# Attention halves that cross a token block are multiplied with v in two pieces

## The chip, the cores and the metric

The kernel runs on one core of one Trainium2 chip. The metric is the device time of one execution in microseconds (us). It was 1517.95 us in the middle of three runs (1516.6 to 1519.84). A core has five engines with instruction queues of their own: TensorE (PE; its weight loads stand apart as PEld), VectorE (DVE), ScalarE (ACT), GpSimd (POOL) and SyncE (SP). They wait for one another by semaphores.

## The reference

```python
# q, k, v: (8 batches, 8 heads, 576 tokens, 64), k and v averaged over groups of 8 tokens: 72 keys
k_p = k.reshape(B, H, Sp, pool, D).mean(axis=3)
v_p = v.reshape(B, H, Sp, pool, D).mean(axis=3)
attn = softmax(scale * q @ k_p.T)            # per head, 576 x 72
x = (attn @ v_p)                             # to (4608 tokens, 512)
h = ((x @ w1) * (x @ w2)) @ w3               # 512 -> 1024 -> 1024
x2 = h @ w_out                               # 1024 -> 512
out = relu(x2 @ w_in) ** 2 @ w_out2          # 512 -> 2048 -> 512
```

## The kernel before

The tokens of all eight batches stand behind one another, 4608 in all. The dense layers take them in nine blocks of `TB = 512` (the loop over `i` near L1383). For each block `stage_ab(i, u)` makes eight times 24 products of 512 columns (tile `ps_w`: x with w1 and with w2), and `stage_w(i, u)` eight times 12 more (tile `acc`). Every operand is a pair of rounded halves, high and low, so that a product takes three matmuls (`mm3`). When all blocks are through, from some 810 us on, the second network follows (tiles `ps_a` to `ps_d`, `ps_h`, `o`).

Attention makes the x of these blocks while they are worked on. A batch has 576 tokens, so its borders fall elsewhere than those of the blocks. It is cut into five tiles of 128, 128, 128, 96 and 96 tokens (`QT`), and these into two halves of 256 and 320 tokens (`HALF`). `pe_s` makes the scores of a tile, `pe_t` turns the softmax, and `pe_av(b, hf, hp)` multiplies a half of a batch with v for one of four pairs of heads: four matmuls as wide as the half (three at L194, one at L533) into one buffer of the tile `ps_av`. ACT copies the result out as the high part of x (L546), and DVE takes the difference as the low part (L549), each once for every block that the half touches. `ps_av`, `ps_s`, `ps_t` and `ps_kt` share a pool of two PSUM buffers (`ps_at`), so that a product has to wait until the one two places ahead in that pool is read out.

`build_tasks` writes the order of these tasks as a list. `attend` is called at every tick of the dense work, about once in six matmuls, and takes tasks from the head of the list against a credit. A task has conditions: `("v", b)` says that v of the batch is split, and `("ab", last - 2)` that the block two before the last one that this half reaches is through `stage_ab`, since x has buffers for two blocks. While the head of the list has to wait, nothing behind it runs, and the credit stops at 3. Where a block is to begin and its x isn't there, `until(lambda: tokens_ready(...))` ticks until the tasks have been issued. A scheduler then moves instructions within a queue, but the order of a list's tasks stays.

v is summed over groups of eight tokens on DVE (L329, and L325 for the rows left over) into `vp` and `v5`, and then split by `cut` and `cut_odd` (L362, L363, L375) into `vl` and `vr`, which `pe_av` loads as weights. Each batch's steps for k and v wait in the list `back["kv"]`, of which `load_back` takes one at a tick. `load_v(b + 1)` is called behind the last product of batch b, and both the sums and the split follow from there.

Of the kernel before, what the change touches and what calls it, by code (L numbers as in the profile page):

```python
# [35 lines left out]
def attn_moe_moe2_kernel(  # L36
# [320 lines left out]
    def load_v(b):  # L357


        def parted(hi, lo, src, row):  # L360

            nc.scalar.activation(hi, src, ACTF.Copy, scale=row)  # L362
            nc.vector.scalar_tensor_tensor(  # L363
                lo, src, row, f32(hi), op0=ALU.mult, op1=ALU.subtract)

        def cut():
            for x in range(2):
                parted(vl[:, 0, :, x, :], vl[:, 1, :, x, :], vp, rows[:, x:x + 1])

        def cut_odd():  # L370
            vo = vr.rearrange("p (a b) t d -> p b a t d", a=2)[:, :, :, 1]
            for x in range(2):
                row = rows[:RB, 2 + x:3 + x]
                parted(vo[:RB, x], vo[2 * RB:, x], v5, row)
                nc.scalar.activation(vo[RB:2 * RB, x], v5, ACTF.Copy, scale=row)  # L375
            done.add(("v", b))

        return kv_parts(v, b, lambda j: vp[:, j, :], [cut, cut_odd])

    def pe_kt(b, part):  # L380

# [140 lines left out]
        dl = rem[RB:2 * RB, :, c0:c0 + n]  # L522
        nc.vector.tensor_sub(dl, ps[RB:2 * RB, :2, :n], f32(dl))

    def pe_av(b, hf, hp):
        hi, lo, rem = atts[b, hf]
        s0 = QT[HALF[hf][0]][0]
        w = sum(QT[i][1] for i in HALF[hf])
        ps = ps_at.tile([P, TB], F32, tag="at", name="ps_av")
        st = [vl[:, i, hp].rearrange("p a d -> p (a d)") for i in range(2)]  # L530
        for m in mm3(ps[:, :w], [(st, [t[:, hp, :w] for t in (hi, lo)])], last=False):
            m()
        nc.tensor.matmul(  # L533
            ps[:, :w], vr[:, hp].rearrange("p a d -> p (a d)"), rem[:, hp // 2, :w],
            start=False, stop=True)
        t0 = b * S + s0
        pieces = []
        o = 0
        while o < w:
            blk, c = divmod(t0 + o, TB)  # L540
            n = min(w - o, TB - c)
            pieces.append((blk, c, o, n))
            o += n

        for blk, c, o, n in pieces:
            nc.scalar.copy(xt_tile(blk, hp)[:, 0, c:c + n], ps[:, o:o + n])  # L546
        for blk, c, o, n in pieces:
            t = xt_tile(blk, hp)
            nc.vector.tensor_sub(t[:, 1, c:c + n], ps[:, o:o + n], f32(t[:, 0, c:c + n]))  # L549
        done.add(("av", b, hf, hp))  # L550

    NG = B * len(QT)

    def s_end(hf):
        return QT[HALF[hf][-1]][0] + QT[HALF[hf][-1]][1]

    def build_tasks(first_k, first_v):
# [4 lines left out]
        pend = []  # L562
        ride = []

        def put(fn, need=()):
            with_it = ride[:]
            del ride[:]
            order.append((need, [*with_it, fn]))

        def close():  # L570
            ends.add(len(order))
# [13 lines left out]
            close()  # L585

        def sc(g):
            alone = not pend
            for half in range(2):
                put(lambda half=half: pe_s(g, half))  # L590
                put_pend()
                if not alone:
                    close()
            close()
# [31 lines left out]
        for g in range(NG):  # L626
            b, i = divmod(g, len(QT))
            hf = 0 if i in HALF[0] else 1

            if g + 1 != len(QT):  # L630
                ahead_of(g)
            if i == HALF[hf][0]:
                put_all()
            for part in range(2):
                put(lambda g=g, part=part: pe_t(g, part))
            close()
            if g == 0:
                for fn in first_v:
                    put(fn)
                    close()  # L640
            if i == HALF[hf][-1]:
                need = [("v", b)]

                last = (b * S + s_end(hf) - 1) // TB
                if last >= 2:
                    need.append(("ab", last - 2))
                for hp in range(NP):
                    def av(b=b, hf=hf, hp=hp):
                        pe_av(b, hf, hp)
                        if hf == 1 and hp == NP - 1 and b + 1 < B:  # L650
                            load_v(b + 1)
                    pend.append((av, need))
                if b < EARLY:
                    put_all()
            if g + 1 == len(QT):
                ahead_of(g)
        put_all()
        return [(need, fns, n + 1 in ends) for n, (need, fns) in enumerate(order)]

    credit = [0.0]  # L660
    rate = [0.0]
# [2 lines left out]
    def attend():  # L664
# [2 lines left out]
        if credit[0] < visit[0]:  # L667
            return
        while credit[0] >= 1.0 and tasks:
            need, fns, ends = tasks[0]  # L670
            if not all(x in done for x in need):
                credit[0] = min(credit[0], 3.0)
                return
            tasks.pop(0)
            for fn in fns:
                fn()
            credit[0] -= 1.0
            if ends and visit[0] > 1:
                return

# [1 line left out]

    def tokens_ready(n):

        b, s = divmod(n, S)
        halves = [(bb, h) for bb in range(b) for h in range(2)]
        if s:
            halves.append((b, 0))
            if s > QT[HALF[1][0]][0]:
                halves.append((b, 1))  # L690
        return all(("av", bb, h, hp) in done for bb, h in halves for hp in range(NP))


    wt = {}
# [822 lines left out]
```

## Time and profile before

| | |
|---|---|
| median of three runs | 1517.95 us |
| the profiled execution: its own time | 1518.94 us |
| its span, from the first to the last instruction | 1517.2 us |
| PE busy | 1478.1 us (97%), 6752 matmuls |
| DVE, ACT, POOL busy | 997.3, 796.5, 81.8 us |
| mean granted TensorE clock | 0.996 of 2.4 GHz |

The profile is of one execution. A matmul's record holds the time that its columns take and the time until its last result is written, so that records of consecutive matmuls overlap; how fast PE goes is read from their starts. Times in the rows below are us from the span's start, if nothing else is said.

### The profile page before, as it was taken

What the parts mean: (1) busy time and instruction counts of PE and PEld (TensorE: products, weight loads), DVE (VectorE), ACT (ScalarE), POOL (GpSimd) and SP (SyncE); (2) the same over time, 40 slices, a digit from 0 to 9 for tenths busy, and PEclk for the clock granted to TensorE, in tenths of its full rate; (3) what the DMA queues carried; (4) which work ended last, traced back from release to release, by engine and by line L of the source; (5) the groups of instructions that cost most, each with busy time, mean ns of one, the idle gap of its engine ahead of it and who ended that gap; (6) DMA issues with size and microseconds to landing.
All of it is one profiled execution on the core that took longest, in us unless ns stands there. A gap on an engine that the chain in (4) does not pass through costs nothing.

```text
span 1517.2 us, 21303 instructions
## 1 busy us (share of the span) xinstructions
PE 1478.1 (97%) x6752; PEld 1199.4 (79%) x6752; DVE 997.3 (66%) x1798; ACT 796.5 (53%) x1953; POOL 81.8 (5%) x145
## 2 busy tenths in 40 slices
PE   5899999999999999999999999999999999999998
PEld 3457788888888887878888888888888888888887
DVE  7988766867666467484256487659675967576542
ACT  6876555546445436463146674456445644554431
POOL 1011111111110011100000000000000000000000
PEclk9999999999999999999999999999999999999999
DMA  9544766758577557475349877778777877798752
GB/s 288 200 140 116 198 184 158 217 141 236 144 202 205 167 138 213 128 243 171 97 146 324 284 201 240 207 208 233 232 208 209 230 207 208 208 271 283 210 161 88
DMA packets 292783, 301.34 MB, mean 199 GB/s; under 512 B 119360, under 2 KB 184896, under 8 KB 292672
## 3 DMA queue, kind: packets, MB, share of 16 engines
q1 hardware_dynamic: 287488, 290.54, 65.8%
q10 hardware_dynamic: 5184, 9.44, 1.7%
q8 instruction: 55, 0.90, 0.3%
q14 instruction: 56, 0.46, 0.1%
HBM read 243.27 MB, written 56.62 MB: 198 GB/s over the span
## 4 chain that ended last, share of the span: by engine, by line
PE 64%; DVE 3%; ACT 3%; issue 1%; DMA 1%; SPq 0%; DVEq 0%; ACTq 0%
PE o L1228 18%; PE ps_w L194 13%; PE acc L194 7%; PE ps_c L1126 5%; PE ps_a L1126 5%; PE ps_d L1126 5%; PE ps_h L194 3%; PE o L194 3%; PE ps_b L1126 3%; PE ps_av L194 1%; PE ps_s L468 1%; DVE gt L122 1%; ACT x2o L121 0%; ACT gs L1134 0%; ACT gt L121 0%
## 5 line engine op out<-in xcount | busy, mean ns | idle before, releaser
L1228 PE MATMUL o<-gt,un 128*128 128x512 f32 x1344 | 329.2, 390 | 0.4
L1228 PEld LDWEIGHTS o<-gt,un 128*128 128x128 f32 x1344 | 251.9, 188 | 54.5 <-DVE gt L122 2.1
L122 DVE TENSOR_TENSOR gt<-gs,gt 128x512 fp32r<-128x512 f32 x240 | 164.5, 688 | 178.9 <-ACT gt L121 177.5
L194 PE MATMUL ps_w<-x,wt 128*128 128x512 f32 x960 | 236.5, 396 | 1.6 <-ACT asb L849 0.7
L121 ACT CAST gt<-gs 128x512 fp32r<-128x512 f32 x240 | 148.5, 620 | 155.0 <-PE o L1228 88.2
L194 PE MATMUL acc<-gt,Wt 128*128 128x512 f32 x864 | 217.8, 396 | 0.0
L194 PEld LDWEIGHTS ps_w<-x,wt 128*128 128x128 f32 x960 | 177.5, 189 | 38.5 <-DVE wt L1319 1.5
L194 PEld LDWEIGHTS acc<-gt,Wt 128*128 128x128 f32 x864 | 160.3, 189 | 31.2
L194 PE MATMUL ps_w<-x,un 128*128 128x512 f32 x768 | 184.7, 393 | 0.0
L194 PEld LDWEIGHTS ps_w<-x,un 128*128 128x128 f32 x768 | 142.6, 188 | 29.0
L485 ACT ACTIVATE att<-ps_s,mx 128x72 f32<-128x72 f32 (+1 forms) x320 | 97.6, 324 | 50.6 <-DVE mx L483 49.7
L1133 ACT ACTIVATE r<-r 128x512 f32<-128x512 f32 x96 | 60.7, 632 | 117.5 <-DVE r L1163 117.0
L853 DVE TENSOR_TENSOR gf<-asb,ps_w 128x512 f32<-128x512 f32 x72 | 49.3, 684 | 84.7 <-PE ps_w L194 84.0
L1126 PE MATMUL ps_d<-x2o,un 128*128 128x512 f32 x384 | 97.4, 389 | 0.0
L1126 PE MATMUL ps_a<-x2o,un 128*128 128x512 f32 x384 | 97.4, 389 | 0.0
L1126 PE MATMUL ps_c<-x2o,un 128*128 128x512 f32 x384 | 97.4, 389 | 0.0
L1134 ACT ACTIVATE gs<-r 128x512 f32<-128x512 f32 x144 | 89.9, 629 | 1.9 <-ACT r L1133 0.2
L121 ACT CAST gt<-gf 128x512 fp32r<-128x512 f32 x72 | 44.9, 624 | 85.6 <-DVE gf L853 85.6
L1202 DVE TENSOR_TENSOR gs<-gs 128x512 f32<-128x512 f32 x128 | 86.4, 683 | 0.0
L1126 PEld LDWEIGHTS ps_a<-x2o,un 128*128 128x128 f32 x384 | 72.1, 188 | 15.0
L1126 PEld LDWEIGHTS ps_d<-x2o,un 128*128 128x128 f32 x384 | 72.1, 188 | 15.0
L1126 PEld LDWEIGHTS ps_c<-x2o,un 128*128 128x128 f32 x384 | 72.1, 188 | 15.0
(114 smaller groups left out, 1964.3 us busy)
## 6 DMA issues: line engine op xcount, KB each, us to landing
un<-u_w SPq DMA_DIRECT2D x128, 256.0 KB, 3.3
un<-u_A SPq DMA_DIRECT2D x128, 256.0 KB, 3.0
un<-u_S SPq DMA_DIRECT2D x128, 256.0 KB, 3.1
un<-u_oS SPq DMA_DIRECT2D x128, 256.0 KB, 3.0
un<-u_oA SPq DMA_DIRECT2D x96, 256.0 KB, 3.0
raw<-in_moe_w_dram SPq DMA_DIRECT2D x32, 512.0 KB, 5.1
raw<-in_moe_w_out_dram SPq DMA_DIRECT2D x24, 512.0 KB, 5.2
kv<-in_k_dram SPq DMA_DIRECT2D x32, 256.0 KB, 3.5
```

Source lines behind the costliest of these rows:

```text
L121: nc.scalar.copy(hi, src)
L122: return (eng or nc.vector).tensor_sub(lo, src, f32(hi))
L194: (lambda a=a, b=b, i=i: nc.tensor.matmul(ps, a, b, start=first and i == 0, stop=last and i == n - 1))
L468: nc.tensor.matmul(ps[:n, x * 2 * SP:(x + 1) * 2 * SP], t[:, hp, c0:c0 + n], kbd[:, hp].rearrange("p a s -> p (a s)"), start=True, stop=True)
L485: nc.scalar.activation(av[:, h0 + h], sv[:, h], ACTF.Exp, bias=mx[:n, h:h + 1], scale=scale, accum_out=sm[:n, h0 + h:h0 + h + 1])
L853: front["dve"] = nc.vector.tensor_mul(gf, asb, pss[1])
L1126: nc.tensor.matmul(ps, l, r, start=first and j == 0, stop=j == len(todo) - 1, skip_group_check=True)
L1133: nc.scalar.activation(t, src, ACTF.Relu)
L1134: nc.scalar.activation(take(name), t, ACTF.Square)
L1202: d = nc.vector.tensor_sub(src, a, src)
L1228: nc.tensor.matmul(ob[x][o], l, r, start=u == 0 and m != 5 and j == 0, stop=u == NU - 1 and j == 2, skip_group_check=True)
```

## The change

A half whose tokens lie on both sides of a block's end, where the later block is the third or a later one, is cut there into two pieces (`av_pieces`). `pe_av` makes one piece, with buffer, matmuls and copies of its own, and each piece has only the `ab` condition of its own block. A piece counts half against the credit. The pieces of six of the sixteen halves are so made (widths in columns): 192 and 128 (batch 1), 128 and 192 (batch 2), 64 and 256 (batch 3), 192 and 64 (batch 5), 128 and 128 (batch 6), 64 and 192 (batch 7). That makes 24 products two each: 96 matmuls and 96 weight loads more, 6848 of each. The copies on ACT and DVE were already cut at the block's end and stay as many.

In `sc`, where a piece heads the list, waiting pieces are put ahead of the scores in twos, and the scores then stand without a product between them. `tokens_ready` asks for the pieces below a token. And v of the next batch but one is loaded and summed as soon as v of the next is split, and it is split directly behind the last product of a batch (`read_v`) where its sums are there, else with the last of them (`summed`).

```diff
@@ load_v
             done.add(("v", b))
-
-        return kv_parts(v, b, lambda j: vp[:, j, :], [cut, cut_odd])
+            if b + 1 < B:
+                load_v(b + 1)
+
+        def summed():
+            done.add(("vs", b))
+            if b in cut_now:
+                cut()
+                cut_odd()
+
+        cuts_v[b] = [cut, cut_odd]
+        return kv_parts(
+            v, b, lambda j: vp[:, j, :], [cut, cut_odd] if b == 0 else [summed])
+
+    cuts_v = {}
+    cut_now = set()
+
+    def read_v(b):
+
+        if b + 1 == B:
+            return
+        cut_now.add(b + 1)
+        if ("vs", b + 1) in done:
+            for fn in cuts_v[b + 1]:
+                fn()
...
+    def av_pieces(b, hf):
+
+        t0 = b * S + QT[HALF[hf][0]][0]
+        w = sum(QT[i][1] for i in HALF[hf])
+        cut = TB - t0 % TB
+        if cut >= w or (t0 + cut) // TB < 2:
+            return [(0, w)]
+        return [(0, cut), (cut, w - cut)]
+
+    def pe_av(b, hf, hp, q0, w):
...
-        for m in mm3(ps[:, :w], [(st, [t[:, hp, :w] for t in (hi, lo)])], last=False):
+        for m in mm3(ps[:, :w], [(st, [t[:, hp, q0:q0 + w] for t in (hi, lo)])], last=False):
...
-            alone = not pend
+            if pend and pend[0][2] < 1:
+                for _ in range(2):
+                    put_pend(2)
+                    close()
+            alone = not pend or pend[0][2] < 1
...
+                pieces = av_pieces(b, hf)
+                for q0, w in pieces:
+                    need = [("v", b)]
+                    last = (b * S + QT[HALF[hf][0]][0] + q0 + w - 1) // TB
+                    if last >= 2:
+                        need.append(("ab", last - 2))
+                    for hp in range(NP):
+                        def av(b=b, hf=hf, hp=hp, q0=q0, w=w, at_end=q0 + w == s_end(hf) - QT[HALF[hf][0]][0]):
+                            pe_av(b, hf, hp, q0, w)
+                            if hf == 1 and hp == NP - 1 and at_end:
+                                read_v(b)
+                        pend.append((av, need, 1.0 / len(pieces)))
...
-            credit[0] -= 1.0
+            credit[0] -= cost
...
+                for q0, w in av_pieces(b, hf):
+                    if t0 + q0 < n and any(
+                            ("av", b, hf, hp, q0) not in done for hp in range(NP)):
+                        return False
```

The first place is PE's queue where block 7 begins, with the first half of batch 7. Before, the four products stand between the last matmuls of `stage_w` for block 6 (`acc`); these are the first two of them, with the scores (`ps_s`) of the next tile.

```order
L194 MATMUL ps_av<-aT_6678,vl 128x256
L533 MATMUL ps_av<-aR,vr 128x256
L468 MATMUL ps_s<-kbd,qT 96x144 x2
L194 MATMUL acc_6420<-gt,Wt 128x512 x3
L194 MATMUL acc_6421<-gt,Wt 128x512
L194 MATMUL ps_av<-aT_6678,vl 128x256
L194 MATMUL ps_av<-aT_6679,vl 128x256
L194 MATMUL ps_av<-aT_6678,vl 128x256
L533 MATMUL ps_av<-aR,vr 128x256
L194 MATMUL acc_6421<-gt,Wt 128x512 x2
```

The same place after the change: the end of `stage_ab` for block 6 (`ps_w`), and the first pieces of 64 columns, two at a time.

```order
L194 MATMUL ps_w_6951<-x_3_5362,un 128x512 x3
L194 MATMUL ps_av<-aT_6773,vl 128x64
L194 MATMUL ps_av<-aT_6774,vl 128x64
L194 MATMUL ps_av<-aT_6773,vl 128x64
L563 MATMUL ps_av<-aR,vr 128x64
L194 MATMUL ps_av<-aT_6773,vl 128x64
L194 MATMUL ps_av<-aT_6774,vl 128x64
L194 MATMUL ps_av<-aT_6773,vl 128x64
L563 MATMUL ps_av<-aR,vr 128x64
L194 MATMUL acc_6478<-gt,Wt 128x512 x3
L194 MATMUL acc_6479<-gt,Wt 128x512 x3
L490 MATMUL ps_s<-kbd,qT 96x144 x4
```

The part of the half that block 7 needs is issued ahead of its border and is narrower. The second pieces come inside block 7's first `stage_ab`, and six matmuls of 512 columns part one pair of them from the next:

```order
L194 MATMUL ps_av<-aT_6773,vl 128x192
L563 MATMUL ps_av<-aR,vr 128x192
L194 MATMUL ps_w_7049<-x_2_6245,wt 128x512 x3
L194 MATMUL ps_w_7049<-x_3_6253,wt 128x512 x3
L194 MATMUL ps_av<-aT_6773,vl 128x192
```

Both parts moved: the first up, ahead of the border, the second down, into block 7. The second place is ACT's queue at the split of v for batch 4, in block 3. Before, it stands some way behind the evictions of the products, behind the exponentials of a tile (L485) and a copy of `ps_w` (`asb`).

```order
L546 CAST x_3_2849<-ps_av 128x64
L546 CAST x_3_3736<-ps_av 128x256
L121 CAST aT_3768<-ps_t 128x4x128
L521 CAST aR<-ps_t 96x2x128
L936 CAST oq<-sq 128x512
L849 COPY asb<-ps_w_3759 128x512
L121 CAST gt<-gf 128x512
L485 ACTIVATE att_104,sm<-ps_s,mx 128x72 x8
L849 COPY asb<-ps_w_3852 128x512
L362 ACTIVATE vl<-vp,rows 128x4x64 x2
```

And after the change:

```order
L576 CAST x_2_3799<-ps_av 128x256
L362 ACTIVATE vl<-vp,rows 128x4x64
L576 CAST x_3_3807<-ps_av 128x256
L362 ACTIVATE vl<-vp,rows 128x4x64
L362 ACTIVATE vr<-v_99,rows 32x2x64
L375 ACTIVATE vr<-v_99,rows 32x2x64
L362 ACTIVATE vr<-v_99,rows 32x2x64
L375 ACTIVATE vr<-v_99,rows 32x2x64
L886 COPY asb<-ps_w_3765 128x512
```

The six activations of the split now follow the last eviction at once, ahead of the copy of the block's first `ps_w`.

## Rows read from the trace of the kernel before

**Rows 1.** The profile's page: busy us (share of the span) and instructions of each engine.
```profile
PE 1478.1 (97%) x6752; PEld 1199.4 (79%) x6752; DVE 997.3 (66%) x1798; ACT 796.5 (53%) x1953; POOL 81.8 (5%) x145
```
**Rows 2.** Windows: stretch, its length, busy us (instructions) of each engine, granted clock, DMA share, GB/s.
```profile
354.00:365.00 11.00, 10.77 (x58) 8.85 (x57) 10.08 (x25) 5.32 (x21) 2.25 (x4) 1.00 0.83 248
435.00:445.00 10.00, 9.37 (x49) 8.04 (x48) 8.41 (x19) 5.82 (x18) 1.58 (x1) 1.00 0.97 290
505.50:515.00 9.50, 9.46 (x54) 7.95 (x54) 4.70 (x16) 4.39 (x19) 1.62 (x3) 1.00 0.64 192
...
672.00:676.00 4.00, 4.00 (x16) 3.47 (x15) 3.01 (x9) 2.23 (x13) 1.15 (x1) 0.57 0.84 306
```
**Rows 3.** Waits: engine line <- releaser: us in total, times, longest.
```profile
ACT x L546 <- PE ps_av L533: 31.2, 29, 3.3
...
PE ps_av L194 <- DVE x L549: 5.6, 5, 2.2
```
**Rows 4.** Timeline of PE, start of block 2: start, length, matmuls, idle before.
```profile
276.25 1.65 PE L194 MATMUL acc<-gt,Wt 128*128 128x512 f32 x6
278.98 0.68 PE L194 MATMUL ps_av<-aT,vl 128*128 128x320 f32 x3 [1.08 <-DVE x L549]
```
**Rows 5.** Timeline of PE, start of block 6.
```profile
586.33 0.66 PE L468 MATMUL ps_s<-kbd,qT 128*96 128x144 f32 x4
586.72 0.95 PE L194 MATMUL acc<-gt,Wt 128*128 128x512 f32 x3
589.19 0.60 PE L194 MATMUL ps_av<-aT,vl 128*128 128x256 f32 x3 [1.52 <-DVE x L549]
```
**Rows 6.** Timeline of PE and DVE, start of block 7.
```profile
666.48 0.51 PE L194 MATMUL ps_av<-aT,vl 128*128 128x256 f32 x3
...
666.83 0.28 PE L533 MATMUL ps_av<-aR,vr 96*128 96x256 f32 x1
...
667.34 1.19 PE L194 MATMUL acc<-gt,Wt 128*128 128x512 f32 x4
...
670.12 0.48 DVE L549 TENSOR_TENSOR x<-ps_av,x 128x64 fp32r<-128x64 f32 x2
...
670.74 0.59 PE L194 MATMUL ps_av<-aT,vl 128*128 128x256 f32 x3 [2.22 <-DVE x L549]
...
671.17 0.28 PE L533 MATMUL ps_av<-aR,vr 96*128 96x256 f32 x1
...
671.29 2.56 PE L194 MATMUL acc<-gt,Wt 128*128 128x512 f32 x7
...
671.96 0.49 DVE L549 TENSOR_TENSOR x<-ps_av,x 128x64 fp32r<-128x64 f32 x2
...
673.65 0.84 PE L194 MATMUL ps_av<-aT,vl 128*128 128x256 f32 x3
...
675.65 1.55 PE L194 MATMUL ps_w<-x,wt 128*128 128x512 f32 x6
```
**Rows 7.** Timeline of PE, start of block 1: products of 320 columns.
```profile
194.74 0.60 PE L194 MATMUL ps_av<-aT,vl 128*128 128x320 f32 x3
195.18 0.31 PE L533 MATMUL ps_av<-aR,vr 96*128 96x320 f32 x1
```
**Rows 8.** The chain that ended last, a dense stretch: start, length, what.
```profile
482.36 5.44 PE ps_w L194 x24
```
**Rows 9.** Timeline of PE's weight loads (PEld) at a turned tile.
```profile
186.00 0.31 PEld L515 LDWEIGHTS ps_t<-ident,att 96*128 96x128 f32 x3
186.25 0.21 PEld L520 LDWEIGHTS ps_t<-ident,rem 96*96 96x96 f32 x2
```
**Rows 10.** The same weight loads, a shorter window.
```profile
186.41 0.30 PEld L194 LDWEIGHTS ps_w<-x,wt 128*128 128x128 f32 x2
```
**Rows 11.** Instructions that touch `ps_av`: ns min/median/max, first and last start.
```profile
L194 PEld LDWEIGHTS ps_av<-aT,vl x192: 186/188/330, 64.0 to 705.1; 128*128 128x128 f32 x192
```
**Rows 12.** Instructions of L362, the split of v, in the same columns.
```profile
L362 ACT ACTIVATE vl<-vp,rows x16: 493/508/562, 49.8 to 648.4; 128x256 fp32r<-128x256 f32 x16
```

More of the change, by code (lines that the diff above doesn't have):

```diff
@@ L523, in pe_t @@
         nc.vector.tensor_sub(dl, ps[RB:2 * RB, :2, :n], f32(dl))
-    def pe_av(b, hf, hp):
+    def av_pieces(b, hf):
[6 more added lines that the diff above has]
+    def pe_av(b, hf, hp, q0, w):
         hi, lo, rem = atts[b, hf]
-        s0 = QT[HALF[hf][0]][0]
-        w = sum(QT[i][1] for i in HALF[hf])
+        s0 = QT[HALF[hf][0]][0] + q0
         ps = ps_at.tile([P, TB], F32, tag="at", name="ps_av")
         st = [vl[:, i, hp].rearrange("p a d -> p (a d)") for i in range(2)]
-        for m in mm3(ps[:, :w], [(st, [t[:, hp, :w] for t in (hi, lo)])], last=False):
+        for m in mm3(ps[:, :w], [(st, [t[:, hp, q0:q0 + w] for t in (hi, lo)])], last=False):
             m()
         nc.tensor.matmul(
-            ps[:, :w], vr[:, hp].rearrange("p a d -> p (a d)"), rem[:, hp // 2, :w],
+            ps[:, :w], vr[:, hp].rearrange("p a d -> p (a d)"), rem[:, hp // 2, q0:q0 + w],
             start=False, stop=True)
@@ L549, in pe_av @@
             nc.vector.tensor_sub(t[:, 1, c:c + n], ps[:, o:o + n], f32(t[:, 0, c:c + n]))
-        done.add(("av", b, hf, hp))
+        done.add(("av", b, hf, hp, q0))
     NG = B * len(QT)
@@ L563, in build_tasks, with put @@
         ride = []
-        def put(fn, need=()):
+        def put(fn, need=(), cost=1.0):
             with_it = ride[:]
             del ride[:]
-            order.append((need, [*with_it, fn]))
+            order.append((need, [*with_it, fn], cost))
         def close():
@@ L587, in sc @@
         def sc(g):
-            alone = not pend
+            if pend and pend[0][2] < 1:
[3 more added lines that the diff above has]
+            alone = not pend or pend[0][2] < 1
             for half in range(2):
                 put(lambda half=half: pe_s(g, half))
-                put_pend()
+                if not alone:
+                    put_pend()
                 if not alone:
@@ L641, in build_tasks @@
             if i == HALF[hf][-1]:
[L642 to L652, printed above, removed]
+                pieces = av_pieces(b, hf)
[10 more added lines that the diff above has]
+                        pend.append((av, need, 1.0 / len(pieces)))
                 if b < EARLY:
@@ L657, in build_tasks @@
         put_all()
-        return [(need, fns, n + 1 in ends) for n, (need, fns) in enumerate(order)]
+        return [(*task, n + 1 in ends) for n, task in enumerate(order)]
     credit = [0.0]
@@ L669, in attend @@
         while credit[0] >= 1.0 and tasks:
-            need, fns, ends = tasks[0]
+            need, fns, cost, ends = tasks[0]
             if not all(x in done for x in need):
@@ L683, in tokens_ready @@
     def tokens_ready(n):
[L685 to L691, printed above, removed]
+        for b in range(B):
+            for hf in range(2):
+                t0 = b * S + QT[HALF[hf][0]][0]
+                for q0, w in av_pieces(b, hf):
+                    if t0 + q0 < n and any(
+                            ("av", b, hf, hp, q0) not in done for hp in range(NP)):
+                        return False
+        return True
     wt = {}
```

## The prediction

> **What bounds the kernel now.** I read the page's busy times first: PE is busy 97% of the span, DVE 66%, ACT 53% [rows 1]. So each added matmul is paid for unless PE stood idle anyway, and each removed stop of PE is a gain. The second view is a table of windows, of which the rows around four block borders and one short stretch are kept: the reader is to see how little idle there is, 0.23 us of 11 at block 3, 0.63 of 10 at block 4, 0.04 of 9.5 at block 5 [rows 2]. Third come the waits: PE waits for one thing in this part more than for others, products (`ps_av`) for DVE's read-out of an earlier product, five times, 5.6 us [rows 3]. The timelines then show where: at the starts of blocks 2, 6 and 7 [rows 4 to 6].
>
> Idle time in these rows understates a stop, since a matmul's record runs on for a while after its columns. I count from starts instead. A matmul of 512 columns holds PE for 5.44 / 24 = 0.227 us [rows 8], one of 320 for (195.18 - 194.74) / 3 = 0.147 [rows 7], one of 256 for (666.83 - 666.48) / 3 = 0.117 [rows 6].
>
> **What it removes.** Before a block starts, the whole half that reaches into it is multiplied in a burst, because the half's condition also asks for the block before. The four products share two buffers with the scores, so the second waits for the first's read-out.
>
> Block 2: six matmuls from 276.25 would end at 277.61, the product starts at 278.98: 1.4 us [rows 4]. Block 6: three from 586.72 would end at 587.40, the product starts at 589.19: 1.8 [rows 5]. Block 7: four from 667.34 would end at 668.25, the product starts at 670.74: 2.5. Behind that stop the granted clock is 0.57 in the mean of four us, so PE runs at the lower of its two levels, 1.2 GHz, for a part of them [rows 2]: seven matmuls from 671.29 take 2.36 instead of 1.59, and two products and one matmul from 673.65 take 2.00 instead of 8 x 0.117 + 0.227 = 1.16 [rows 6]. That is 1.6 more. Blocks 3 and 5 show 0.3 us of idle time together, and block 1 none; I take 0.5 for all three. Block 4 starts just where a half ends, so no half is cut there and its stop stays. The sum is 1.4 + 1.8 + 2.5 + 1.6 + 0.5 = 7.8 us.
>
> With the new order every border's products are issued before it, in the pieces that need nothing of the later block. So I count all of the 7.8 as gone, and ask below what takes its place. The earlier sums of v help to this end, since a product also asks for v; no wait in these rows names v, so they get no time of their own.
>
> **What it adds on PE.** 24 products become two each. Their columns stay the same, and if columns were all, the price would be the fixed part of 96 matmuls: (0.227 - 0.117) / 256 is 0.00043 us a column, which leaves 0.007 a matmul, 0.7 us in all. But each matmul loads its own 128 x 128 weights, and the next load runs beside the matmul before it. Two such loads that follow one another directly, with no long matmul to hide in, span 0.30 us, one alone 0.19 [rows 10, 11]: the second starts 0.11 behind the first. Matmuls of 64, 128 or 192 columns, which by columns take 0.03 to 0.09, then come every 0.11 us. For four head pairs of four matmuls, 16 in a half, I get:
>
> batches 1 and 2 (192 and 128 for 320 columns): 2 x 0.11 - 0.147 = 0.073 each;
> batch 3 (64 and 256 for 320): 0.11 + 0.117 - 0.147 = 0.080;
> batches 5, 6 and 7 (two short ones for 256): 2 x 0.11 - 0.117 = 0.103 each.
>
> 16 x (2 x 0.073 + 0.080 + 3 x 0.103) = 8.6 us. No row shows a rounded matmul under 256 columns, so the bounds are wide. Below stands the 0.7 of columns alone. Above stands the pace of the plain f32 scores: four records of 144 columns from 586.33 to 586.72, two for each product, so some 0.195 us a product and 0.00135 a column [rows 5]. At that pace 64 columns keep 0.11, 128 take 0.174 and 192 take 0.260: 16 x (2 x (0.260 + 0.174 - 0.147) + 0.080 + 2 x (0.260 + 0.11 - 0.117) + (0.348 - 0.117)) = 22 us. I take 8.6, since its row is of the same operation and size of weights.
>
> The Trainium skill speaks of this in "TensorE: Matmul & The Clock Gate", section "Back-to-back issue gap": for a stream of weight loads and matmuls it gives about 81 ns a matmul at 128 columns. By that the added time would be some 4 us, an estimate. The trace's own 0.11 is longer than that for rounded operands, and the measured one stands in the sum; the shorter pace is a rival below, priced from a row.
>
> **What it adds as waits.** The pieces stand in pairs. Eight of the twelve pairs that follow another pair of the same pieces are parted from it by six matmuls of 512, four by twelve. The third piece needs the first's buffer. From the start of the first piece's last matmul there are 0.55 us to the next long matmul and 6 x 0.227 = 1.36 to the third piece, 1.91, of which 0.28 is that matmul's own record: 1.63 us for the read-out. The trace shows both kinds: the product that ends at 671.45 is read out at 672.45, 1.0 us later, the one that ends at 667.11 at 670.60, 3.5 later, because other casts stood ahead of it [rows 6]. So a pair waits 0 to 1.9 us, and eight of them 0 to 15. ACT was idle and waited for the product in 29 cases [rows 3], so most read-outs are quick, and pieces have shorter ones; I take 0.25 a pair, 2.0 us. With twelve matmuls between there are 3.0 us, and I take nothing.
>
> **What it moves at no cost.** Sums, split and loads of v stay as many. The loads, 256 KB each on SP's queue, start about a batch earlier, into the same three buffers, and the sums take a place in DVE's queue that has a third of its time free. The split is the step to watch, since it now stands in one run behind the last read-out on ACT: two activations of 0.51 us and four smaller ones, at most 3.1 us [rows 12]. Behind them waits the copy of the block's first `ps_w`, and for that PE's third group of 12 matmuls. PE has at least 24 matmuls of 512 ahead of that one, 5.4 us, against 3.1 + 0.6 for the copy: hidden, by PE's own work. Were that cover gone, the price would be some 3 us a block, 18 in all. The products themselves become no more for DVE or ACT, since their copies were in pieces before.
>
> **The sum.** 1517.2 - 7.8 + 8.6 + 2.0 = 1520.0 us of span. 1.7 us lie around the span (1518.94 in all), which gives 1521.7. The profiled execution is 1.0 above the median of the three runs, so against these I predict 1520.7 us, 2.8 more. A difference within 0.2%, 3.0 us, is what a measurement can't tell from none.
>
> **Rivals.**
>
> Short pieces come faster. In the turned tiles, loads of 128 columns of weights follow one another every 0.25 / 3 = 0.083 us [rows 9]. If pieces keep that pace, 64 and 128 columns cost 0.083 and 192 cost 0.090, and the added time is 16 x (2 x 0.026 + 0.053 + 2 x 0.056 + 0.049) = 4.3: 1516.4 us. If columns alone count and no pair waits, 1510.8. Against it: those tiles are plain f32 and turned, and their loads have shorter records. It ends on the faster side if the pace is under 0.08 or if small stops elsewhere go too.
>
> Late read-outs, the slower side: the second pieces stand where ACT and DVE still work off the block before (its `gt`, converted weights, the split of v). If each of the eight pairs meets a read-out like the 3.5 us one, PE waits 15 us: 1533.7. It decides from read-outs over 1.6 us. Against it: 1.0 is the commoner figure.
>
> Pieces at the plain f32 pace: 22 instead of 8.6 gives 1534. Speaking for it is only that narrow rounded matmuls are unseen here; the 256-column ones show no sign of it.
>
> The change doesn't do what it says: the stops come from conversions on ACT and DVE that fall on the border, and they stay with whatever product is there. Then the 7.8 isn't saved: 1528.5. The 3.5 us read-out speaks for it, but there are six matmuls to hide in now where there were three or four.
>
> **How the numbers follow.** My forecast has a chance of 0.54, and a range of its own from 1517 to 1525; within it 0.03 falls to faster, 0.31 to same, 0.20 to slower. Faster pieces have 0.24, half of it over the bound: 0.13 faster, 0.11 same. Late read-outs have 0.10, the f32 pace 0.06, no saving 0.06, all slower. Together that is 0.16 faster, 0.42 same, 0.42 slower. The range of 1513 to 1529 leaves out most of the f32 pace, half of the late read-outs and the far end of the fast pieces, under 0.2.
>
> **What would show it.** Starts of matmuls with 64, 128 and 192 columns 0.11 us apart would bear out the main term; 0.03 to 0.09, or more than 0.2 at 128, would refute it. The waits of products for DVE at the starts of blocks 2, 6 and 7 should be gone, with the stretch at the lower clock, while block 4's stays. New ones should stand ahead of the third piece of a pair, a quarter of a microsecond each. A loss of more than 8 us, or a gain of more than 5, would mean that one of the two large terms is wrong.

## The result and the profile after

The changed kernel took 1525.9 us in the middle of five runs (1524.91 to 1527.31), the kernel before 1517.95. The ratio is 1.0052, with an interval of 1.0042 to 1.0063: slower by 0.5%, some 8 us where 2.8 were forecast. It lies in the range given, and 0.9 us above the forecast's own (1517 to 1525). The profiled execution is the one of 1525.9 us; its span is 1524.1, 6.9 more than before.

The page answers to [rows 1]:

```profile
PE 1486.2 (98%) x6848; PEld 1209.0 (79%) x6848; DVE 1001.2 (66%) x1798; ACT 795.6 (52%) x1953; POOL 84.4 (6%) x145
```

96 matmuls and weight loads came on top, nothing else did. In the windows view, the block starts of [rows 2] stand here at other times (block 3 at 359.6, block 4 at 438.0, block 5 at 515.5, block 7 at 677.6 us); the fifth row is a new place. Columns as there: stretch, length, busy us of PE, PEld, DVE, ACT, POOL, granted clock, DMA share, GB/s.

```profile
358.50:369.50 11.00, 10.58 (x57) 8.78 (x56) 9.33 (x22) 7.87 (x25) 1.89 (x3) 1.00 0.94 280
438.00:448.00 10.00, 10.00 (x53) 8.70 (x52) 4.26 (x11) 4.68 (x17) 1.15 (x1) 1.00 0.56 175
515.00:524.50 9.50, 9.50 (x55) 8.19 (x54) 2.79 (x8) 2.19 (x7) 0.47 (x2) 1.00 0.03 9
674.00:678.00 4.00, 4.00 (x22) 3.41 (x22) 1.93 (x6) 1.55 (x9) 0.00 (x0) 1.00 0.24 73
465.00:479.00 14.00, 11.79 (x57) 9.87 (x56) 11.27 (x26) 6.09 (x20) 0.00 (x0) 0.88 0.63 152
```

The starts of blocks 4, 5 and 7 have no idle time left, block 3's has more than before (0.42 us, where it was 0.23), and block 7's clock is full, where it was 0.57. But inside block 4, at 465 to 479, PE idles 2.2 us and the clock falls. The timeline of PE where block 7 begins answers to [rows 6]:

```profile
669.30 0.42 PE L194 MATMUL ps_av<-aT,vl 128*128 128x64 f32 x3
669.55 0.28 PE L563 MATMUL ps_av<-aR,vr 96*128 96x64 f32 x1
669.66 0.50 PE L194 MATMUL ps_av<-aT,vl 128*128 128x64 f32 x3
670.00 0.28 PE L563 MATMUL ps_av<-aR,vr 96*128 96x64 f32 x1
670.11 3.01 PE L194 MATMUL ps_w<-x,un 128*128 128x512 f32 x12
672.96 0.41 PE L194 MATMUL ps_av<-aT,vl 128*128 128x64 f32 x3
...
675.24 1.14 PE L490 MATMUL ps_s<-kbd,qT 128*96 128x144 f32 x8
676.12 1.64 PE L194 MATMUL acc<-gt,Wt 128*128 128x512 f32 x6
```

The second product's three matmuls span 670.00 - 669.66 = 0.34 us, 0.113 each; the first product's, right behind a long matmul, span 0.25. Over all pieces the median from start to start is 0.110 to 0.112 us at 64, 128 and 192 columns alike, against 0.118 at 256 and 0.146 at 320. The pairs at 669.30 and 672.96 follow without a stop.

The waits of PE answer to [rows 3] (engine line <- releaser: us in total, times, longest):

```profile
PE ps_av L194 <- DVE x L579: 2.7, 4, 1.3
PE ps_s L490 <- DVE x L579: 2.4, 2, 2.2
...
PE ps_t L542 <- DVE x L579: 1.3, 1, 1.3
```

All three name the same releaser, the subtraction by which DVE reads a product out and frees its buffer (L579, before L549). The products' own waits are halved, 5.6 to 2.7, but the scores and the turned tiles, which share the two buffers, now wait for it too. The longest is at 474.73. Three timelines, of PE, ACT and DVE, show what happens there:

```profile
470.86 0.27 PE L563 MATMUL ps_av<-aR,vr 96*128 96x192 f32 x1
470.97 1.55 PE L194 MATMUL ps_w<-x,wt 128*128 128x512 f32 x6
474.73 2.00 PE L490 MATMUL ps_s<-kbd,qT 128*96 128x144 f32 x8 [2.21 <-DVE x L579]
476.36 2.08 PE L194 MATMUL ps_w<-x,wt 128*128 128x512 f32 x4
```

```profile
470.95 0.67 ACT L152 ACTIVATE rq<-rq 128x512 f32<-128x512 f32 x1 [0.49 <-DMA qraw<-in_q_dram]
471.52 0.66 ACT L153 ACTIVATE wq<-rq 128x512 uint32<-128x512 uint32 x1
472.07 0.30 ACT L576 CAST x<-ps_av 128x192 fp32r<-128x192 f32 x1
474.16 0.62 ACT L973 CAST oq<-wq 128x512 fp32r<-128x512 f32 x1 [1.78 <-issue]
474.69 0.31 ACT L576 CAST x<-ps_av 128x192 fp32r<-128x192 f32 x1
```

```profile
472.67 0.69 DVE L162 SCALAR_TENSOR_TENSOR rq<-rq 128x512 uint32<-128x512 uint32 x1
473.39 0.69 DVE L164 CUSTOM_DVE_ANT_0 wq<-rq,wq 128x1024 uint16<-128x1024 uint16 x1
474.00 0.44 DVE L468 STREAM_TRANSPOSE qT<-qraw 128x256 f32<-128x256 f32 x1
474.36 0.32 DVE L579 TENSOR_TENSOR x<-ps_av,x 128x192 fp32r<-128x192 f32 x1
```

The two products end near 470.7 and 471.1. ACT copies the first at 472.07 and the second at 474.69: ahead of them in its list stand steps that convert the second network's weights (L152, L153, L973), and L973 needs DVE's L164, which ends at 474.1. DVE's subtraction for the first product stands behind steps of the same conversion (L162, L164) and a transpose of q (L468) and comes at 474.36. So PE stops for 2.2 us, and then works at the lower clock, 1.2 GHz (eight scores take 476.36 - 474.73 = 1.63 us, where they take 676.12 - 675.24 = 0.88 at block 7).

### The profile page after: what moved, and what is told of

The parts are those of the page before. It is cut to its first block, busy times and chain, and to the rows that moved or that the text cites. A ratio compares the mean times of both kernels' runs of the same rounds, so it can differ in the third digit from the quotient of the medians.

```text
span 1524.1 us, 21467 instructions
## 1 busy us (share of the span) xinstructions
PE 1486.2 (98%) x6848; PEld 1209.0 (79%) x6848; DVE 1001.2 (66%) x1798; ACT 795.6 (52%) x1953; POOL 84.4 (6%) x145
## 4 chain that ended last, share of the span: by engine, by line
PE 83%; DVE 6%; ACT 4%; DMA 4%; SPq 2%; issue 1%; DVEq 0%; ACTq 0%
PE ps_w L194 23%; PE o L1265 18%; PE acc L194 12%; PE ps_a L1163 5%; PE ps_c L1163 5%; PE ps_d L1163 5%; PE ps_h L194 3%; PE o L194 3%; PE ps_b L1163 3%; PE ps_s L490 2%; PE ps_av L194 1%; PE ps_t L537 1%; DMA raw<-in_moe_w_dram 1%; DVE raw L162 1%; ACT att L507 1%
```

## The experiments

Most readings below use one sum. For each pair of matmuls that follow one another on PE, I take the time between their starts, and the median of that time over all matmuls of the same line and shape. The medians added up are the work at its pace; what goes beyond is stops and stretches at the lower clock. (Some 13 to 14 us before the first and behind the last matmul's start are in neither.) The kernel before was run again beside each group of kernels, with medians of 1517.59 to 1518.18 us; the ratios are against those.

| kernel | median us | ratio to before, 95% | at pace, us | beyond, us |
|---|---|---|---|---|
| before | 1517.95 | 1 | 1451.6 | 51.4 |
| after | 1525.9 | 1.0042 to 1.0063 | 1461.0 | 49.8 |
| e1, v alone | 1510.67 | 0.9936 to 0.996 | 1451.6 | 42.9 |
| e2, cut alone | 1543.77 | 1.0151 to 1.0177 | 1461.1 | 68.0 |
| e3, columns cut, one buffer | 1549.09 | 1.0185 to 1.0211 | 1463.6 | 71.5 |
| e4, three halves cut | 1521.53 | 1.0016 to 1.0043 | 1456.1 | 49.2 |
| e5, quiet border | 1514.72 | 0.9967 to 0.9985 | 1451.6 | 48.8 |
| e6, e5 and e3's columns | 1539.8 | 1.0133 to 1.0165 | 1460.6 | 63.4 |
| e9, conversions put off | 1525.17 | 1.004 to 1.007 | 1460.3 | 52.2 |
| e10, v's sums alone early | 1515.95 | 0.9976 to 0.9997 | 1451.5 | 48.0 |
| e11, e6 with sums behind | 1531.8 | 1.0082 to 1.0114 | 1460.5 | 53.2 |
| e13, after, conversions behind | 1522.69 | 1.0016 to 1.0043 | 1460.3 | 51.0 |
| e14, e1, all behind | 1517.91 | 0.999 to 1.0007 | 1451.6 | 50.6 |
| e15, e13 from the first block on | 1517.52 | 0.9991 to 1.0008 | 1460.3 | 42.9 |

The last two columns are of the profiled execution alone. That of e13 is the slowest of its twelve, that of e11 the fastest of its six.

**e1: v's part without the cut.** The changed kernel, in which no half is cut:

```diff
     def av_pieces(b, hf):
...
-        if cut >= w or (t0 + cut) // TB < 2:
+        if True:
             return [(0, w)]
```

> No half is cut; v is summed and split as after the change. Theory (the cut's extra weight loads and the read-outs of its pairs are the loss, v's part is worth little by itself): the products still stand in a burst ahead of blocks 1, 2, 3, 5, 6 and 7, the stops of the kernel before stay but for a part at block 6, so 1516 to 1519 us. Rival (the split of v, now in one run among the read-outs on ACT, is the loss): 1521 us or more.

It took 1510.67 us, 7.3 less than before and the fastest of all the kernels here: both the theory and the rival missed it. The work at its pace is that of before to 0.1 us; 8.5 us of stops and lower clock are gone, 4.1 of them between the starts of blocks 6 and 7, 1.6 between those of 1 and 2, 1.0 between those of 5 and 6. Another 2.7 lie between the starts of blocks 0 and 1, where the kernel before has the lower clock for 3.4 us behind a stop at 138 us that both kernels have, and no stop at the border; between the other blocks 0.8 is lost. Of ACT, the first four rows here are of the kernel before at the start of block 7, the last one is of e1:

```profile
666.97 0.62 ACT L936 CAST oq<-sq 128x512 fp32r<-128x512 f32 x1 [0.56 <-DMA u_oA<-oq]
667.49 0.62 ACT L121 CAST gt<-gf 128x512 fp32r<-128x512 f32 x1
668.34 1.25 ACT L153 ACTIVATE wq<-raw 128x512 uint32<-128x512 uint32 x2 [0.23 <-DVE oq L940]
669.49 0.41 ACT L546 CAST x<-ps_av 128x64 fp32r<-128x64 f32 x2
```

```profile
662.00 0.43 ACT L576 CAST x<-ps_av 128x64 fp32r<-128x64 f32 x2 [0.34 <-PE ps_av L563]
```

Before, the first product of this half ended at 667.11 [rows 6], while a conversion (L936) was under way, and a cast and two more conversions stood ahead of its read-out at 669.49: 2.4 us. In e1 the same product ended at 661.96 and is read out at 662.00, with no conversion ahead of it. The last activation that splits v into `vl` starts at 634.5 there, against 648.4 before [rows 12]. So whole halves need not stop PE at the border; stops of 0.5, 1.1 and 0.7 us are left at blocks 2, 5 and 6.

The other two long stops of the kernel before have the same form. The row pairs are DVE's at blocks 2 and 6:

```profile
277.55 1.02 DVE L329 TENSOR_REDUCE kp<-kv 128x64 f32<-128x512 f32 x1 [0.69 <-DMA kv<-in_k_dram]
278.49 0.35 DVE L549 TENSOR_TENSOR x<-ps_av,x 128x192 fp32r<-128x192 f32 x1
```

```profile
587.95 0.69 DVE L940 TENSOR_TENSOR oq<-sq,oq 128x512 fp32r<-128x512 f32 x1
588.56 0.48 DVE L549 TENSOR_TENSOR x<-ps_av,x 128x128 fp32r<-128x128 f32 x2
```

At block 2 the second part of a subtraction stands behind a sum of k that waits for its load, at block 6 a subtraction stands behind a conversion (L940).

**e2: the cut without v's part.** Pieces as in the change; v is loaded, summed and split as before:

```diff
-            if b + 1 < B:
-                load_v(b + 1)
...
-            v, b, lambda j: vp[:, j, :], [cut, cut_odd] if b == 0 else [summed])
+            v, b, lambda j: vp[:, j, :], [cut, cut_odd])
...
                             if hf == 1 and hp == NP - 1 and at_end:
-                                read_v(b)
+                                if b + 1 < B:
+                                    load_v(b + 1)
```

> Halves are cut as after the change; v is loaded, summed and split as before it. Theory: the 8.6 us of weight loads and the read-outs stay, the wait behind v's split (1.5 us at 286 us in block 2) goes, but v comes late for the first pieces at blocks 3 and 7 and PE stops there: 1524 to 1528 us. Rival (v's part is the loss): 1520 us or less.

1543.77 us, 25.8 above before, which no theory had. With pieces ahead of a border, products need v earlier than it is split. A row of PE at batch 5:

```profile
489.91 0.33 PE L561 MATMUL ps_av<-aR,vr 96*128 96x192 f32 x1 [0.52 <-ACT vr L375]
```

But that is the smaller part: of PE's waits here 3.5 us name v and 8.2 a late read-out, and the lower clock follows four times in the blocks. The cut does worse without the other half of the change: with v early it costs 15.2 us over e1, without it 25.8 over before.

**e3: the short matmuls by themselves.** The kernel before; a half that crosses is multiplied as two runs of columns into the same buffer, so that only the 96 matmuls are new:

```diff
+        cut = TB - t0 % TB
+        whole = cut >= w or (t0 + cut) // TB < 2
+        for q0, n in [(0, w)] if whole else [(0, cut), (cut, w - cut)]:
+            for m in mm3(ps[:, q0:q0 + n], [(st, [t[:, hp, q0:q0 + n] for t in (hi, lo)])], last=False):
+                m()
...
```

> The kernel before, its order and its read-outs, but the six crossing halves are multiplied in the same two column pieces within one buffer: 96 matmuls and weight loads more and nothing else. Theory (a matmul under 256 columns is paced by its weights, 0.11 us): 8.6 us more than before, less what of it falls into stops that PE makes anyway, so 1523 to 1527 us. Rival (columns alone): 0.7 us more, 1518.7. Rival (the cut's loss is all in waits): within 2 us of the kernel before.

1549.09 us, 31 above before: as a price of the matmuls this missed. At their pace they cost 12.0 us in this run, part of it at the lower clock (its mean was 0.987); 20 us are longer stops at the same borders as before and the lower clock behind them. From block 1 on the granted clock is 0.50 for 34 us (from 282, 371, 610 and 695 us on), where before it is so for 3.4. By the eight scores above, 1.63 us at the lower clock and 0.88 without, near half of such time is lost; by estimate that is some 14 of the 31 us. e6 and e11 look for what makes such stops.

**e4: three of the six halves cut.** Those of batches 2, 6 and 7, v as in the change:

```diff
-        if cut >= w or (t0 + cut) // TB < 2:
+        if cut >= w or b not in (2, 6, 7):
```

> Only the halves of batches 2, 6 and 7 are cut, those whose bursts stopped PE before by 1.4, 1.8 and 4.1 us; v as after the change. Theory: 16 x (0.073 + 0.103 + 0.103) = 4.5 us of weight loads instead of 8.6, and the stop at 475 us (some 4 us with the lower clock) goes with the pieces of batch 5, while some 0.5 us of stops come back: 1516 to 1520 us. Rival (read-outs queue by chance and stop PE elsewhere as long): 1521 to 1523 us.

1521.53 us, as the rival had it. The working of the prediction gives these three halves 16 x (0.073 + 2 x 0.103) = 4.5 us; the pace column shows 1456.1 - 1451.6 = 4.5. The other 6.3 us over e1 are stops; the longest, 2.6 us at 509, is at block 5, whose half is whole here, and its read-out stands behind four conversions on DVE.

**e5: a quiet border.** The kernel before; while a block's start waits for products, no other background work is issued:

```diff
-        until(lambda: tokens_ready((i + 1) * TB))
+        alone_until(lambda: tokens_ready((i + 1) * TB))
...
+    def alone_until(cond):
+        n = 0
+        while not cond():
+            left = len(tasks)
+            ticks[0] += 1
+            attend()
+            n += 1
+            if len(tasks) == left and n > 4:
+                tick()
...
```

> The kernel before, changed in one thing: while a block's start waits for its products, only the tasks (products, scores) are issued; the sums of k and v, the conversions of the second network's weights and the other work of each tick wait until the block has begun. No half is cut and v stands as before. Theory (the stops at block starts are read-outs that stand behind sums and conversions on ACT and DVE, not the halves themselves): the stops of 1.4, 1.8 and 2.5 us at blocks 2, 6 and 7 shrink to about 0.5 each and the stretch at the lower clock goes, so 4 to 6 us less: 1512 to 1514. Rival (two buffers alone set the stops, whatever stands beside them): 1517 to 1519. Second rival (the work that is put off meets the next read-outs): slower, 1519 to 1523.

1514.72 us, 3.0 less than the kernel before, run beside it. The direction is the theory's, and the size is short of it: the stop at block 7 fell from 2.4 us to two of 0.75 and block 6's is gone, but block 2's fell only from 1.25 to 0.98, where DVE still has sums of k ahead of the read-out.

**e6: e3 on that footing.**

> The previous kernel (e5), in which besides each of the 24 products of a half that reaches over a block's end is multiplied as two column pieces into the same buffer: 96 matmuls more, the same products, read-outs and waits. It is the price of the short pieces with the background out of the burst. Theory (0.11 us a matmul under 256 columns, as the starts of the changed kernel's pieces show): e5 plus 8.6 us, within 1.5. Rival (each product of pieces also makes its read-out later, so that the stops grow again as in e3, where the same edit cost 31 us): e5 plus 15 or more.

1539.8 us, 25 over e5: the rival's side. The pace column gives 1460.6 - 1451.6 = 9.0 for the matmuls; the rest, 14.6 in the profiled executions, is stops, the largest of 4.1 us at block 2, and the lower clock behind them (0.50 for 17 us, from 281 and 691 on; by the same estimate some 8). DVE there:

```profile
278.14 0.67 DVE L133 TENSOR_TENSOR gt<-gf,gt 128x512 fp32r<-128x512 f32 x1
278.74 1.94 DVE L340 TENSOR_REDUCE kp<-kv 128x64 f32<-128x512 f32 x2
281.19 1.01 DVE L340 TENSOR_REDUCE vp<-kv 128x64 f32<-128x512 f32 x1 [0.52 <-DMA kv<-in_v_dram]
282.12 0.54 DVE L563 TENSOR_TENSOR x<-ps_av,x 128x128 fp32r<-128x128 f32 x2
```

The product ended near 277.1. Its subtraction (L563) stands behind the sums from 278.74 on, two of k and one of v, the last of which waits for its load. In e5's list these three stand behind the subtraction. The edit touched neither the sums nor the subtraction; the scheduler put the queue in another order. (The next expectation says three sums of k; it is two.)

**e11: the sums held behind the read-outs.** e6, and

```diff
-            nc.vector.tensor_sub(t[:, 1, c:c + n], ps[:, o:o + n], f32(t[:, 0, c:c + n]))
+            front["dve"] = nc.vector.tensor_sub(
+                t[:, 1, c:c + n], ps[:, o:o + n], f32(t[:, 0, c:c + n]))
```

after which a later sum of k or v is issued behind this subtraction.

> The kernel e6 with one thing more: each sum of k or v is put behind the last read-out of a product that was issued ahead of it, on DVE, which works through its list in order. In e6 three sums of k and one of v, each waiting for its load, stand in DVE's list ahead of the subtraction that frees the first product's buffer at block 2, and PE stops there for 4.1 us; in e5 they stand behind it. Theory (e6's 25 us over e5 are 8.6 us of short matmuls, and for the rest the place of sums ahead of read-outs): a gain of 4 to 10 us over e6, 1530 to 1536, and no stop over 2 us at block 2. Rival (the short pieces themselves cost PE the 25 us): 1538 to 1541.

1531.8 us, 8.0 less, as the theory had it. The same rows of DVE now:

```profile
276.20 0.68 DVE L133 TENSOR_TENSOR gt<-gf,gt 128x512 fp32r<-128x512 f32 x1
276.80 0.54 DVE L563 TENSOR_TENSOR x<-ps_av,x 128x128 fp32r<-128x128 f32 x2
```

The stop of 4.1 us is gone (1.0 is left, for the exponentials on ACT). So of the 25 us in e6 some 9 are the pace of the short matmuls and 8 the place of sums. In what is left a third thing shows, at block 7 of e11 (columns as in the windows above):

```profile
675.90:686.20 10.30, 10.30 (x40) 9.19 (x41) 8.01 (x24) 7.42 (x25) 1.15 (x1) 0.50 0.69 246
```

PE has no idle time in these 10.3 us, and the granted clock is 0.50 all the while. Ahead of them stand two waits for the split of v, of 1.0 and 0.6 us; in them stand most of the half's short matmuls; behind them, in the long matmuls of block 7, the clock is full again. By the same estimate that costs some 5 us, as much as everything that e11's profiled execution has beyond its pace over e5's (53.2 - 48.8 = 4.4). Whether the short matmuls hold the clock there or the stops ahead of them do, no run parts. That e3's stops have the causes found in e6 is argued, not shown.

**e9: conversions put off.** The changed kernel; a step of the conversions is not issued in a tick near pieces, and made up for later:

```diff
...
+        near = ticks[0] <= piece_at[0] + 1 or (
+            tasks and tasks[0][2] < 1 and all(x in done for x in tasks[0][0]))
+        if due[0] and not near:
+            due[0] -= 1
+            run_step(quarters)
```

> The changed kernel, in which a step of the conversions of the second network's weights is put off while pieces are next in the list of tasks or were issued in this or the last tick, and made up for afterwards. Cut and v as in the changed kernel. Theory (PE's new waits at 266, 364, 475 and 600 us, some 8 us with the lower clock behind them, are read-outs of pieces that stand behind such conversions): 5 to 8 us less, 1518 to 1521. Rival (the conversions only move to other read-outs and the total stays): 1524 to 1528.

1525.17 us: the theory missed, the rival held. PE's long waits stayed (2.0 us at 281 and 473, 2.4 at 601). By its time alone this run speaks against the conversions as the cause. Its trace does not. ACT at the wait at 473:

```profile
471.12 0.66 ACT L152 ACTIVATE rq<-rq 128x512 f32<-128x512 f32 x1 [3.09 <-DMA rq<-in_moe_w_in_dram]
472.23 0.53 ACT L576 CAST x<-ps_av 128x192 fp32r<-128x192 f32 x2
```

The two products ended near 469.4 and 469.9, and ACT sits idle before a conversion that waits for its load, with the read-outs behind it. At 601 conversions stand ahead as well, at 281 a conversion and two sums of k. So the edit left them where they hurt. A tick only sets when an instruction is written down, and the scheduler still chooses its place in the queue; the next run sets the place.

**e13: conversions held in the queues.** The changed kernel, in which each converting instruction on ACT or DVE is issued behind the last read-out written ahead of it (eleven places, of which one is shown, and two that mark the read-outs):

```diff
...
+            front["av_act"] = nc.scalar.copy(xt_tile(blk, hp)[:, 0, c:c + n], ps[:, o:o + n])
...
-            nc.scalar.copy(order(t[:, 0, :]), natural(part(n)))
+            after_av("act", nc.scalar.copy(order(t[:, 0, :]), natural(part(n))))
```

> The changed kernel, in which the instructions that convert the second network's weights are put, on ACT and on DVE, behind the last read-out that was issued ahead of them. Cut, v and the issue of each tick as in the changed kernel. e9 put the conversions off by ticks, and the waits stayed. Theory (the waits at 266, 364, 475 and 600 us come from conversions that stand ahead of read-outs in the lists of ACT and DVE): 4 to 8 us less than the changed kernel, 1518 to 1522. Rival (the read-outs are late for other reasons, exponentials, v's split, the loads): 1524 to 1528.

1522.69 us (1517.8 to 1527.35), 3.2 less than the changed kernel and just short of the theory. The waits at 364 and 600 are gone, those at 266 and 475 shrank to 0.5 each, and from the start of block 1 to that of block 8 it takes 549.4 us against 555.1. But the profiled execution, the slowest, lost 5 us at the start. PE and POOL there:

```profile
103.86 0.48 PE L422 MATMUL ps_kt<-ident,kp 128*128 128x128 f32 x1 [3.56 <-POOL kp L357]
```

```profile
100.69 3.11 POOL L357 COPY kp<-kp 64x64 f32<-64x64 f32 x1 [1.84 <-DVE kp L334]
```

PE waits for a copy of k's sums that takes POOL 3.11 us; in the changed kernel the same copy starts at 100.73 and takes 0.37. The lower clock follows (0.50 from 102.1 to 108.8). Six converting steps run on DVE beside the copy in both kernels, so these rows don't tell why it is slow here, nor whether the order of the conversions makes it so.

**e15: the same from the first block on.**

```diff
-        if "av_" + eng in front:
+        if "on" in front and "av_" + eng in front:
...
     rate[0] = 0.7
+    front["on"] = True
```

> As e13, but the conversions are put behind the read-outs only from the first block on; the start, where e13 stopped PE for 5 us more at 99 to 104 us (its block 0 starts at 120.6 us against the changed kernel's 115.6), is as in the changed kernel. Theory (conversions ahead of read-outs make the changed kernel's new waits; e13 takes 5.7 us less than it from block 1's start to block 8's and gave them back at the start): 5 to 7 us less than the changed kernel, 1519 to 1521. Rival (e13's gain in the blocks hung on its late start): 1523 to 1527.

1517.52 us, 8.4 less than the changed kernel, a little more than the theory had, and no different from the kernel before. In the profiled executions 6.3 us of the gain lie between the starts of blocks 1 and 8 (548.8 against 555.1). Another 1.7 lie ahead of block 0, where the order isn't set yet, and block 0 gives 0.7 back. POOL's copy is short again (0.37 us). The waits of PE, and the place that cost 4 us in the changed kernel (PE, then ACT):

```profile
PE ps_s L495 <- DVE x L584: 0.7, 2, 0.4
PE ps_av L199 <- DVE x L584: 0.6, 2, 0.4
```

```profile
470.64 1.22 PE L495 MATMUL ps_s<-kbd,qT 128*96 128x144 f32 x8 [0.42 <-DVE x L584]
```

```profile
469.90 0.51 ACT L581 CAST x<-ps_av 128x192 fp32r<-128x192 f32 x2
470.31 0.62 ACT L979 CAST oq<-wq 128x512 fp32r<-128x512 f32 x1
```

Both read-outs now go ahead of L979 (L973 above), and the wait is 0.42 us at full clock.

**e10: v's sums early, its split not in one run.** No cut; the split's two steps go back into the background list:

```diff
-            for fn in cuts_v[b + 1]:
-                fn()
+            back["kv"][:0] = [((False, b + 1), fn) for fn in cuts_v[b + 1]]
...
```

> No half cut. v's next batch is loaded and summed as early as in the change, but its split is not issued in one run behind the last product: its two steps go into the list of background work there and are issued one a tick, about as before. Theory (the 7.3 us that v's part gave alone come from the early sums, which leave DVE and ACT free for read-outs at the next border): 1510 to 1512. Rival (they come from the split in one run): 1515 to 1518.

1515.95 us, in the rival's range: early sums alone give about 2 of e1's 7.3 us, and with the split directly behind the products it is 7.3. What order that leads to in the queues is part of it; the two aren't parted further.

**e14: e1 with sums and conversions behind read-outs.**

> v as in the change, no half cut (as e1), and both the sums of k and v and the conversions put behind the read-outs on their engines. Theory (e1's remaining stops at 274, 359, 505 and 586 us, 3.0 us together, come from what stands ahead of the read-outs): 1507 to 1510, the fastest of all. Rival (the order within the lists makes no difference without pieces): 1510 to 1512.

1517.91 us, 7 slower than e1, against both the theory and the rival. Its loss is at the start, as in e13: block 0 begins at 120.4 us, in e1 at 114.3, and POOL's copy takes 3.11 us here too, in e1 0.37. From there to the end it takes 1.8 us more than e1, so with whole halves this order of sums and conversions gave nothing to win. It wasn't run without the loss at the start.

## Why the prediction was partly right

**What it adds on PE, 8.6 us: right.** The pace of 0.11 us is measured at all three widths, and the sum comes out at 8.7 in the changed kernel, e9, e13 and e15, 4.5 for half of it in e4. (The table has 9.4 for the changed kernel; 0.7 of that is in 16 small transposes of q, whose median is another there.) That the columns don't set it is shown by 64, 128 and 192 all taking the same. That the weight load does, as I had it, is not shown: in the turned tiles loads of 128 columns follow one another every 0.083 us [rows 9]. The Trainium skill's "TensorE: Matmul & The Clock Gate", section "Back-to-back issue gap", gives about 81 ns at 128 columns; here 0.112 us was measured, and the measurement decides.

**What it removes, 7.8 us: gone, but not for the reason given.** The stops at blocks 2, 6 and 7 and the lower clock at block 7 went as forecast. I put them down to the whole half, multiplied in a burst through two buffers. e1 keeps all halves whole, and 8.5 us of stops and lower clock are gone there, 6 of them in the blocks from 1 on. What stopped PE was sums and conversions ahead of the read-outs in DVE's and ACT's lists, as the rows at blocks 2, 6 and 7 show and e5, in part, by experiment. My fourth rival said that; I gave it 0.06, for the case that the stops stay. They didn't stay: with v's part that work stands elsewhere, though how v's part moves it isn't followed step by step.

**v's part "at no cost and no gain": wrong.** Alone it is worth 7.3 us. It was the step that failed, and the one with no row behind its gain: I asked whether the split would delay something, and not whether v's work, out of the way before the border, would let other work go ahead. The one cost that I looked for is there at another place: at 286.12 a turned tile waits 1.3 us for DVE, since the last read-out of a batch, of a product that ended near 283.0, stands behind four activations of the split, two of them the `vl` here. ACT, DVE and PE there:

```profile
284.28 0.91 ACT L362 ACTIVATE vl<-vp,rows 128x256 fp32r<-128x256 f32 x2
...
285.10 0.30 ACT L576 CAST x<-ps_av 128x192 fp32r<-128x192 f32 x1
...
285.62 0.35 DVE L579 TENSOR_TENSOR x<-ps_av,x 128x192 fp32r<-128x192 f32 x1
...
286.12 0.40 PE L542 MATMUL ps_t<-ident,rem 128*96 128x128 f32 x2 [1.32 <-DVE x L579]
```

**Waits of 2.0 us: the term that was mis-sized.** I took 0.25 us for each of eight pairs. Most pairs wait for nothing, and a few for a lot: by starts, 1.7 us at 266, 0.7 at 364, 1.3 at 600, 0.5 at 202, and some 4 at 475 with the lower clock, 8 in all; e15 takes 6.3 off in the blocks by the order of the conversions alone. The late read-out of 3.5 us in [rows 6] was the row to price them by. I had it as a rival at 1533.7 with a chance of 0.10; the truth lay between.

**Block 4's stop "stays": wrong.** The window 438 to 448 has no idle time. Before, a product waited there at 439.25 for 0.8 us; in e1 0.2 of it is left, so it was v's part that took most of it.

Set against before, the sum was to be -7.8 + 8.6 + 2.0 = 2.8. By the runs it reads: v's part -7.3; the cut on top of it +15.2, of which some 9 are pace and the rest late read-outs and the lower clock behind one of them. That the forecast of 1520.7 came near is luck in part: the gain of 7.8 given to the cut and the nothing given to v's part are both wrong, by about as much, to opposite sides. Most of the miss of 5.2 us that is left is the waits, priced at 2.0. A loss of more than 8 us was to be the sign that a large term is wrong; it was 7.95, and one was. The best form with a cut, e15, ends where the kernel before was, 6.8 us behind e1.

## What to carry to other kernels

A change with two parts is to be priced part by part, each against the wait that it ends; here the gain belonged to the part that looked like bookkeeping, and the cut paid short matmuls for a stop that was none of its own. Where buffers are few, look in the reading engines' lists at what stands ahead of a read-out, and fix its place by an order in the queue: delaying the code that writes an instruction did not do it (e9), and an edit elsewhere can undo it (e6). A read-out that is quick in most cases is to be priced by the share of late ones, not by the usual.

## What was not expected of the hardware and the scheduler

The same 96 matmuls cost some 9 us at their pace (12 in e3, part of it at the lower clock), but 31, 25, 17 or 15 us in all (e3, e6 over e5, e11 over e5, after over e1), by where a scheduler puts sums and conversions on two other engines, and by how long the lower clock lasts. A stop costs more than its length where the lower clock follows: behind the 2.2 us at 474.73 eight scores took 1.63 us instead of 0.88, and four matmuls of 512 columns span 2.08 us where six span 1.55 at 470.97. The lower clock can last without a stop: in e11 for 10.3 us in which PE was never idle. From 64 to 192 columns a matmul with weights of its own costs the same 0.11 us, so that the narrow piece of an uneven cut gets nothing for its width.
